# Heads of a packed attention as 64x32 tiles of the matrix array, and two batches in shared sweeps over d_ff

## The chip, the cores and the metric

The kernel runs on one core of one Trainium2 chip. The metric is device time in microseconds (us) of one launch. TensorE (PE) multiplies matrices, and its weight loads are listed apart as PEld; VectorE is DVE, ScalarE is ACT, GpSimd is POOL, and SyncE (SP) issues all DMAs. Each engine works through its own instructions in order, and semaphores hold it back where it needs another engine's result.

## The reference

For each of 8 batches and 8 heads, 32 packed queries `p` attend over 576 keys and values; the result `p'` then serves as key and value for the 576 real queries. The heads are put side by side (8 x 64 = 512 columns) and go through a feed-forward layer with a PReLU.

```python
def sm_attn(qq, kk, vv):                      # head_dim 64, softmax over the last axis
    s = scale * qq @ kk.T
    s = s - max(s); a = exp(s); a = a / (sum(a) + 1e-09)
    return a @ vv
p_packed = sm_attn(p, k, v)                   # 32 x 64 per head
out      = sm_attn(q, p_packed, p_packed)     # 576 x 64 per head
x = out with heads side by side               # 4608 tokens x 512
h = x @ w_in                                  # 512 x 2048, float64 in memory
g = max(h, 0) + alpha * min(h, 0)
return g @ w_out                              # 2048 x 512, float64 in memory
```

## The kernel before

The second attention's weights (576 tokens x 32 packed rows, 8 heads = 256 rows) are called `a`. Since `out @ w_in = a @ (p' w_in)`, the kernel forms `pw = p' w_in` per batch (256 x 2048) and multiplies `a` by it.

**Steps.** A batch's 576 tokens are two halves of 288 columns; `k` = 0 to 15 counts the halves of all batches, `f` = 0 to 15 the blocks of 128 columns of d_ff. A *step* (k, f) is `first` (`ps_h` = `pw` block times `a` half; ACT `neg` = relu(-x), line 401; DVE adds `neg` times (1 - alpha), line 402; ACT copies `gh`, line 407; DVE subtracts `gl`, line 408) and, two steps later, `second`: for each of four output blocks three matmuls into `acc` (lines 420 to 422, `wo` high times `gh`, `wo` low times `gh`, `wo` high times `gl`). This splits a float32 operand into a high and a low float32r part, so that three float32r matmuls stand for one in float32. `first` splits in the same way (lines 395 to 397, six matmuls, after `split_pw` on DVE, lines 371 and 373); for batch 0 (`XF = 1`) it uses two unsplit float32 matmuls (line 383). PE's 256 steps run in the order of the list `order`: first k = 0 and 1 in four sweeps of four f each (sums kept in `part` between sweeps), then k = 2, 3, ... with all 16 f.

**Weights.** `w_out` and `w_in` come as float64 in 32 blocks of 128 x 512 (`wraw`, 512 KB each). `convert` makes float32 of one with two ACT passes and four DVE passes (lines 112 to 126), then splits it with one more pass on each (lines 128, 129). `w_in` is written back, split, as `w_split`, and read again for later batches.

**Attention.** `attention(b, tp)` handles two pairs of heads, as a generator whose stages are called at step numbers given by the list `plan`. Scores (line 188): the stationary matrix holds two heads of a pair on the diagonal of 128 rows x 64 columns with zeros elsewhere (`s1f`, `p2f`); two pairs of heads fill the two halves of the output's 128 partitions. p' (line 258) are matmuls of 128 rows x 64 columns in the same way. `packed_w` (lines 350 to 352) forms `pw` of two batches at once, with 128 x 128 stationary matrices that again hold zeros off the diagonal, split into three float32r matmuls of 512 columns, 16 times; ACT copies the results to `pw`. PSUM is shared out as four banks `acc`, two `ps_h`, and two `ps_m` for everything else.

The scheduler of the framework orders each engine's instructions within what data and buffers allow; the code's order and the step numbers give it the priorities.

Of the kernel before, what the change touches and what calls it, by code (L numbers as in the profile page):

```python
# [16 lines left out]


# [10 lines left out]
def pack_attention_ffn_kernel(  # L29
# [17 lines left out]

# [16 lines left out]
    xin = ctx.enter_context(tc.tile_pool(name="xin", bufs=3))  # L66
    vin = ctx.enter_context(tc.tile_pool(name="vin", bufs=2))
    wk = ctx.enter_context(tc.tile_pool(name="wk", bufs=3))
    sm = ctx.enter_context(tc.tile_pool(name="sm", bufs=4))
    at = ctx.enter_context(tc.tile_pool(name="at", bufs=3))  # L70
    pwp = ctx.enter_context(tc.tile_pool(name="pwp", bufs=8))
    pwj = ctx.enter_context(tc.tile_pool(name="pwj", bufs=2))
    win = ctx.enter_context(tc.tile_pool(name="win", bufs=3))
    gp = ctx.enter_context(tc.tile_pool(name="gp", bufs=2))
# [6 lines left out]
    w_split = dram.tile([NJ, NP, P, 2, 512], F32, name="w_split")  # L81

# [5 lines left out]
    pt = const.tile([P, NP, 2, 2, 64], F32R, name="pt")  # L88
    s1f = const.tile([P, NP, 64], F32, name="s1f")
    p2f = const.tile([P, NP, 64], F32, name="p2f")  # L90
    pt0 = const.tile([P, NP, 2, 2, 64], F32R, name="pt0", tag=f"wo{NF - 1}")
    for t in (s1f, p2f, fv(pt0)):
        nc.gpsimd.memset(t, 0.0)
    wo_t = {}

    XF = 1

    def convert(src, raw, place):

# [3 lines left out]
        mag = xin.tile([P, 512], F32, name="mag", tag="xh")  # L110
        bits = mag.bitcast(U32)
        nc.scalar.activation(out=mag, in_=up, func=AF.Abs)
        low = xin.tile([P, 512], U32, name="low", tag="xl")
# [13 lines left out]
        hi, lo = place()  # L127
        nc.scalar.copy(out=hi, in_=mag)  # L128
        nc.vector.tensor_tensor(out=lo, in0=mag, in1=fv(hi), op=ALU.subtract)  # L129

    def new_raw(f=0):

        if f in left:
            left.remove(f)
            n = f
        elif f == NF - 1:
            n = f
        else:
            n = left.pop(0)
            left.append(n)  # L140
        return const.tile([P, 512], U64, name=f"wraw{n}", tag=f"wo{n}")

    SPARE = 4
    left = list(range(NF - 1 - SPARE, NF - 1))

    def load_w_out(f):
        def place():
            wo_t[f] = const.tile([P, 2, DM], F32R, name=f"wo{f}", tag=f"wo{f}")
            return wo_t[f][:, 0, :], wo_t[f][:, 1, :]

        raw = new_raw(f)
        convert(w_out[f * P : (f + 1) * P, :], raw, place)


    def load_x(src, b, pr):
        if b == 0 and (src is kT or pr == NP - 1):
            n = pr if src is kT else 2 * NP
            raw = const.tile([P, S], F32, name=f"xraw{n}", tag=f"wo{n}")
        else:
            raw = xin.tile([P, S], F32, name="xraw", tag="xraw", bufs=3)  # L160
        nc.sync.dma_start(out=raw, in_=src[b, pr])
        return raw

    def load_v(b, pr):
        if b == 0:
            raw = const.tile([P, KT, P], F32, name=f"vraw{pr}", tag=f"wo{NP + pr}")
        else:
            raw = vin.tile([P, KT, P], F32, name="vraw", tag="vraw")
        nc.gpsimd.memset(raw[: KT * P - S, KT - 1, :], 0.0)
        nc.sync.dma_start(  # L170
            out=raw[:, : KT - 1, :],
            in_=v[b, pr, : (KT - 1) * P].rearrange("(kt kp) d -> kp kt d", kp=P),
        )
        nc.sync.dma_start(out=raw[KT * P - S :, KT - 1, :], in_=v[b, pr, (KT - 1) * P :])
        return raw

    def scores(b, prs, st, xs):

        for hf in range(2):
            sl = slice(hf * HS, hf * HS + HS)  # L180
            if b == 0:
                tag = f"acc{(prs[0] + hf) % 4}"
                ps = ps_a.tile([P, 512], F32, name=tag, tag=tag)
            else:
                ps = ps_m.tile([P, 512], F32, name="ps_m", tag="m")
            for pr, x in zip(prs, xs):
                ro = (pr % 2) * 64
                nc.tensor.matmul(ps[ro : ro + 64, :HS], st[:, pr], x[:, sl], start=True, stop=True)  # L188
            yield hf, sl, ps[:, :HS]

    def new_a(b):
        a_h = at.tile([P, 2, S], F32R, name="a_h", tag="a_h")
        a_l = at.tile([P, 2, S], F32R, name="a_l", tag="a_l", bufs=4)
        result[b] = (a_h, a_l)

    def attention(b, tp):

        ptb, slots = (pt0, (0, 1)) if b == 0 else (pt, (b % 2, b % 2))
        pr0, pr1 = prs = (2 * tp, 2 * tp + 1)
        ts = slice(2 * tp, 2 * tp + 2)
        if tp == 0:
            praw = sm.tile([P, NP, N], F32, name="praw", tag="praw", bufs=1)
            nc.sync.dma_start(out=praw, in_=pT[b])
        k0 = load_x(kT, b, pr0)
        k1 = load_x(kT, b, pr1)
        yield  # L210
        if tp == 0:
            for r in range(2):
                rs, cs = slice(r * 64, r * 64 + 64), slice(r * N, r * N + N)
                nc.scalar.copy(out=s1f[rs, :, cs], in_=praw[rs])
        yield
        s_t = wk.tile([P, S], F32, name="s_t", tag="w")
        for hf, sl, ps in scores(b, prs, s1f, (k0, k1)):
            if hf or b > 0:
                nc.scalar.copy(out=s_t[:, sl], in_=ps)
            else:  # L220
                nc.vector.tensor_copy(out=s_t[:, sl], in_=ps)
        vraw = [load_v(b, pr0)]
# [78 lines left out]
        if b not in result:  # L301
            new_a(b)
# [246 lines left out]
```

## Time and profile before

| | |
|---|---|
| median of 3 runs | 818.55 us (816.24 to 819.24) |
| profiled execution | 816.14 us, its span 814.3 us (1.84 us lie around it) |
| PE clock granted, mean | 0.983 |
| busy: PE, PEld, DVE, ACT, POOL | 775.9, 704.7, 538.5, 412.3, 77.4 us |
| first matmul of line 383, of line 420 | 37.1 us, 49.4 us |
| first matmul of `second` for k = 4 | 290.8 us |
| DMA | 97.95 MB in all; 294 GB/s in the first fortieth of the span |

A row of grouped instructions reads: line, engine, operation, output<-inputs, shape, count, then busy time and mean ns of one. In the shape of a matmul, `128*64` are the rows and columns of the array that it uses, and `128x288` the output. A float32 matmul leaves two records, one for each pass; a float32r matmul and a transpose leave one. The duration of a matmul's record includes its way through the pipeline, so the pace of matmuls is read from start to start. A row of stages (windows) gives the stretch, its length, the busy time and instruction count of each engine, the mean PE clock, the DMA share and GB/s.

### The profile page before, as it was taken

To read this page: it belongs to the slowest core of one execution; us is meant where nothing else is said; L and a number is where in the kernel's file an instruction comes from. 1 tells how busy PE (TensorE), PEld (TensorE's weight loads), DVE (VectorE), ACT (ScalarE), POOL (GpSimd) and SP (SyncE) were. 2 spreads that over 40 slices of the span, in tenths; PEclk is the share of its full clock that TensorE was granted. 3 is DMA by queue.
4 is the path that set the end of the run, shared out by engine and by line. 5 is a ranking of instruction groups with operands and counts; after the bars stand their busy time and mean duration, and the time that the engine had idled before them with its cause. 6 is when DMAs were issued, how large, how long until landed. Compare 5 with 4: busy or idle time off the path is not lost.

```text
span 814.3 us, 14561 instructions
## 1 busy us (share of the span) xinstructions
PE 775.9 (95%) x5456; PEld 704.7 (87%) x5456; DVE 538.5 (66%) x1165; ACT 412.3 (51%) x987; POOL 77.4 (10%) x95
## 2 busy tenths in 40 slices
PE   5599887999999999999999999999999999999997
PEld 3268656888889999899999988889999999999997
DVE  3999998755463468775565568675565566666664
ACT  5688756645547654547335554436435533333332
POOL 1000000025243003012000003010100000000000
PEclk9679999999999999999999999999999999999999
DMA  9887665667446523324303223115303000000000
GB/s 294 289 274 259 217 215 185 200 198 222 143 138 230 192 92 117 91 88 163 126 2 133 81 89 118 59 44 181 108 1 107 2 30 1 30 1 31 1 30 30
DMA packets 55382, 97.95 MB, mean 120 GB/s; under 512 B 5136, under 2 KB 32784, under 8 KB 55312
## 3 DMA queue, kind: packets, MB, share of 16 engines
q1 hardware_dynamic: 55312, 97.02, 36.4%
q8 instruction: 43, 0.70, 0.4%
q14 instruction: 27, 0.22, 0.1%
HBM read 79.18 MB, written 17.83 MB: 119 GB/s over the span
## 4 chain that ended last, share of the span: by engine, by line
PE 84%; DVE 10%; DMA 2%; ACT 2%; issue 1%; SPq 0%; POOL 0%; ACTq 0%; DVEq 0%; POOLq 0%
PE acc L420 16%; PE acc L421 15%; PE acc L422 15%; PE ps_h L395 8%; PE ps_h L397 7%; PE ps_h L396 7%; PE ps_m L188 4%; PE ps_h L383 2%; PE ps_m L258 2%; PE ps_m L352 2%; PE ps_m L351 2%; PE ps_m L350 2%; DVE mag L122 2%; DMA wraw<-in_w_out 2%; DVE mag L126 1%
## 5 line engine op out<-in xcount | busy, mean ns | idle before, releaser
L420 PE MATMUL acc<-gh,wo 128*128 128x288 f32 x1024 | 289.6, 300 | 8.4 <-ACT gh L407 6.6
L421 PE MATMUL acc<-gh,wo 128*128 128x288 f32 x1024 | 285.1, 295 | 0.0
L422 PE MATMUL acc<-gl,wo 128*128 128x288 f32 x1024 | 216.2, 301 | 0.0
L420 PEld LDWEIGHTS acc<-gh,wo 128*128 128x128 f32 x1024 | 192.3, 188 | 22.6 <-ACT gh L407 8.9
L421 PEld LDWEIGHTS acc<-gh,wo 128*128 128x128 f32 x1024 | 192.4, 188 | 2.6 <-issue 0.9
L401 ACT ACTIVATE neg<-ps_h 128x288 f32<-128x288 f32 x256 | 105.1, 412 | 162.6 <-PE ps_h L397 149.7
L408 DVE TENSOR_TENSOR gl<-ps_h,gh 128x288 fp32r<-128x288 f32 x256 | 116.0, 455 | 97.1 <-ACT gh L407 95.5
L402 DVE SCALAR_TENSOR_TENSOR ps_h<-neg,nal,ps_h 128x288 f32<-128x288 f32 x256 | 130.9, 516 | 60.1 <-ACT neg L401 59.5
L407 ACT CAST gh<-ps_h 128x288 fp32r<-128x288 f32 x256 | 102.4, 400 | 133.2 <-DVE ps_h L402 132.0
L422 PEld LDWEIGHTS acc<-gl,wo 128*128 128x128 f32 x1024 | 163.4, 188 | 5.2 <-issue 1.3
L395 PE MATMUL ps_h<-a_h,pwh 128*128 128x288 f32 x448 | 134.3, 300 | 0.0
L397 PE MATMUL ps_h<-a_h,pwl 128*128 128x288 f32 x448 | 132.4, 296 | 0.0
L396 PE MATMUL ps_h<-a_l,pwh 128*128 128x288 f32 x448 | 132.2, 295 | 0.0
L371 DVE CAST pwh<-pw 128x512 fp32r<-128x512 f32 x112 | 51.9, 465 | 65.0 <-PE ps_h L396 64.3
L395 PEld LDWEIGHTS ps_h<-a_h,pwh 128*128 128x128 f32 x448 | 84.0, 188 | 6.2 <-issue 5.0
L397 PEld LDWEIGHTS ps_h<-a_h,pwl 128*128 128x128 f32 x448 | 84.1, 188 | 1.2 <-issue 1.0
L396 PEld LDWEIGHTS ps_h<-a_l,pwh 128*128 128x128 f32 x448 | 84.1, 188 | 0.7 <-issue 0.4
L358 ACT COPY pw<-ps_m 64x512 f32<-64x512 f32 x112 | 65.1, 581 | 23.4 <-PE ps_m L352 16.9
L373 DVE TENSOR_TENSOR pwl<-pw,pwh 128x512 fp32r<-128x512 f32 x96 | 70.2, 732 | 7.9 <-PE ps_h L397 0.3
L383 PE MATMUL ps_h<-a_f,pw 128*128 128x288 f32 x128 | 40.8, 438 | 5.5 <-DVE gl L408 3.4
L352 PE MATMUL ps_m<-w,pt 128*128 128x512 f32 (+1 forms) x80 | 33.7, 424 | 4.4 <-DVE w L129 4.4
L350 PE MATMUL ps_m<-w,pt 128*128 128x512 f32 (+1 forms) x80 | 34.2, 427 | 3.6 <-ACT w L128 3.1
(80 smaller groups left out, 695.2 us busy)
## 6 DMA issues: line engine op xcount, KB each, us to landing
w<-w_split SPq DMA_DIRECT2D x64, 512.0 KB, 4.0
xraw<-in_kT SPq DMA_DIRECT2D x32, 288.0 KB, 3.1
xraw<-in_qT SPq DMA_DIRECT2D x32, 288.0 KB, 3.2
outT<-ot SPq DMA_DIRECT2D x64, 144.0 KB, 1.9
vraw<-in_v SPq DMA_DIRECT2D x32, 256.0 KB, 3.3
wraw<-in_w_out SPq DMA_DIRECT2D x16, 512.0 KB, 4.6
wraw<-in_w_in SPq DMA_DIRECT2D x16, 512.0 KB, 4.8
w_split<-w SPq DMA_DIRECT2D x16, 512.0 KB, 3.7
```

The lines of the kernel that those rows point to most:

```text
L358: nc.scalar.copy(out=pw[b, j][ro : ro + 64, pr // 2, :], in_=ps[i * 64 : i * 64 + 64, :])
L373: eng.tensor_tensor(out=tl, in0=src, in1=fv(th), op=ALU.subtract)
L395: nc.tensor.matmul(ps[:, :HS], th[:, i, fs], a_h[:, i, tok], start=hi, stop=False)
L396: nc.tensor.matmul(ps[:, :HS], th[:, i, fs], a_l[:, i, tok], start=False, stop=False)
L397: nc.tensor.matmul(ps[:, :HS], tl[:, i, fs], a_h[:, i, tok], start=False, stop=lo)
L401: nc.scalar.activation(out=neg, in_=g, func=AF.Relu, scale=-1.0)
L402: nc.vector.scalar_tensor_tensor(out=g, in0=neg, scalar=nal[:, f : f + 1], in1=g, op0=ALU.mult, op1=ALU.add)
L407: nc.scalar.copy(out=gh, in_=g)
L408: nc.vector.tensor_tensor(out=gl, in0=g, in1=fv(gh), op=ALU.subtract)
L420: nc.tensor.matmul(acc[o][:, :HS], wo_t[f][:, 0, os_], gh, start=begin, stop=False)
L421: nc.tensor.matmul(acc[o][:, :HS], wo_t[f][:, 1, os_], gh, start=False, stop=False)
L422: nc.tensor.matmul(acc[o][:, :HS], wo_t[f][:, 0, os_], gl, start=False, stop=end)
```

## The change

- **Heads as tiles.** The stationary matrices hold no zeros any more: each head is a tile of 64 rows (its head_dim) and 32 columns (its packed rows). `heads()` runs through eight of them; row half `r` goes to PSUM bank `r`, and pair `pr` to the 32 partitions `pr`. Scores (now line 193) and `packed_w` (line 306) are eight such matmuls each. p' (line 252) is 128 rows x 32 columns with 64 output columns, four side by side. Batches are handled whole, so `attention(b)` has no `tp`.
- **p' w_in in float32.** `packed_w` makes one float32 matmul of 512 columns per head, one batch at a time, in place of three float32r matmuls; `w_in` is kept unsplit (`w_whole`, 256 KB a block). Zero-filled tiles, splits of p' and of `w_in` and the ACT copies of halves fall away; the softmax's 1/sum is applied in the copy of p' (line 256).
- **Sweeps.** Batches 0 and 1 (k = 0 to 3) now share four sweeps of four f: 64 steps. For both, `first` multiplies unsplit in float32 (`XF = 2`, line 345). Sums stay in `part` for four k; the `at` ring (tag `a`, 7 buffers) holds `part` and `a` alike.
- **Order.** Ahead of the steps, `go` calls stages of attention 0 and 1 (`a`, `b`) and conversions of `w_in` (`i`) in a written order. A string `CONV` gives one conversion or one `packed_w` of batches 0 and 1 to each of the first 35 steps; a later batch's attention takes one stage a step from step 32(b-1)+2 on, and its `packed_w` follows from 32(b-1)+21 on. What is called in a step is placed behind that step's last matmul of `first`, `neg` and line 360 (`issue_after`). `split_pw` is on DVE alone. Pools get more buffers.

```diff
+    def heads():
+        for pr in range(NP):
+            for r in range(2):
+                yield pr, r, slice(r * 64, r * 64 + 64), slice(pr * N, pr * N + N)
-    def scores(b, prs, st, xs):
-        for hf in range(2):
...
-            for pr, x in zip(prs, xs):
-                ro = (pr % 2) * 64
-                nc.tensor.matmul(ps[ro : ro + 64, :HS], st[:, pr], x[:, sl], start=True, stop=True)
+    def scores(b, st, xs, hf):
...
+        for pr, r, rs, cs in heads():
+            nc.tensor.matmul(
+                banks[r][cs, :HS], st[rs, cs], xs[pr][rs, hf * HS : hf * HS + HS],
+                start=True, stop=True,
+            )
...
+            for kt in range(KT):
+                for pr in range(NP):
+                    cs = slice(pr * N, pr * N + N)
+                    nc.tensor.matmul(
+                        ps[cs, rs], aT[:, kt, r, cs], vs[pr][:, kt, rs],
+                        start=(kt == 0), stop=(kt == KT - 1),
+                    )
+            nc.scalar.activation(out=c[:, rs], in_=ps[:, rs], func=AF.Copy, scale=dens[r])
...
+    def packed_w(b, j):
+        banks = [bank() for _ in range(2)]
+        for pr, r, rs, cs in heads():
+            nc.tensor.matmul(
+                banks[r][cs, :], p2[b][rs, cs], wi_t[j, pr][rs, :], start=True, stop=True
+            )
+        pw[b, j] = pwp.tile([P, 2, 512], F32, name="pw", tag="pw")
+        for r in range(2):
+            nc.scalar.copy(out=pw[b, j][:, r, :], in_=banks[r])
...
+    XF = 2
+    go("aiiaabiiaaaaabbb")
...
+    go("bbaabb")
+    packed_w(0, 0)
+    drain(a0)
+    SWEEPS = [(f, f + 4) for f in range(0, NF, 4)]
+    order = [(t, f, s) for s in SWEEPS for t in range(4) for f in range(*s)]
+    order += [(k, f, (0, NF)) for k in range(4, 2 * B) for f in range(NF)]
...
+    CONV = "oooo1iiiioooo01iiiioooo01iiii01oooo"
+    add(converted(CONV), [0 + n // 1 for n in range(len(CONV))])
+    add(a1, [n // 2 for n in range(14)])
+    for b in range(2, B):
+        T = 32 * (b - 1)
+        add(attention(b), range(T + 2, T + 2 + 18))
+        add(packed_w_steps(b), [T + 21 + 2 * n for n in range(NJ + 1)])
```

PE, at one block of p' w_in of later batches. Before, for two batches (`pt` holds p' of both), one of 16 such groups of three:

```order
L421 MATMUL acc_4079<-gh,wo_1076 128x288
L422 MATMUL acc_4079<-gl,wo_1076 128x288
L350 MATMUL ps_m<-w,pt 128x512
L351 MATMUL ps_m<-w,pt 128x512
L352 MATMUL ps_m<-w,pt 128x512
L420 MATMUL acc_4076<-gh,wo_1163 128x288
```

And after, for one batch (`p_3214` is its p'), four such places, each with eight tiles:

```order
L355 MATMUL ps_h<-a_h,pwh 128x288
L306 MATMUL ps_m<-w,p_3214 32x512 x8
L377 MATMUL acc_3536<-gh,wo_1265 128x288
L378 MATMUL acc_3536<-gh,wo_1265 128x288
L379 MATMUL acc_3536<-gl,wo_1265 128x288
```

Eight float32 tiles thus stand where three full float32r matmuls stood, in eight groups for two batches instead of 16, with `first` and `second` on either side.

DVE, in the first sweep, where conversions and steps share it. Before:

```order
L402 SCALAR_TENSOR_TENSOR ps_h<-neg,nal,ps_h 128x288
L126 ISA mag<-mag,low 128x1024
L118 TENSOR_SCALAR mag<-mag 128x512
L115 TENSOR_SCALAR mag<-mag 128x512
L408 TENSOR_TENSOR gl<-ps_h,gh 128x288
L122 SCALAR_TENSOR_TENSOR mag<-wraw_541,mag 128x512
L118 TENSOR_SCALAR mag<-mag 128x512
L129 TENSOR_TENSOR w<-mag,w 128x512
L402 SCALAR_TENSOR_TENSOR ps_h<-neg,nal,ps_h 128x288
```

After:

```order
L360 SCALAR_TENSOR_TENSOR ps_h<-neg,nal,ps_h 128x288
L122 TENSOR_SCALAR mag<-mag 128x512
L119 TENSOR_SCALAR mag<-mag 128x512
L367 TENSOR_TENSOR gl<-ps_h,gh 128x288
L126 SCALAR_TENSOR_TENSOR mag<-wraw_852,mag 128x512
L367 TENSOR_TENSOR gl<-ps_h,gh 128x288
L122 TENSOR_SCALAR mag<-mag 128x512
L130 ISA w<-w,low 128x1024
L126 SCALAR_TENSOR_TENSOR mag<-wraw_892,mag 128x512
L360 SCALAR_TENSOR_TENSOR ps_h<-neg,nal,ps_h 128x288
```

The pattern is alike; only the block of `w_in` has lost its last pass (`w<-mag,w`, line 129).

SP's queue before the first step, after the change (`w_whole<-w` waits for a converted block, and `in_qT` behind it is batch 0's):

```order
L160 DMA xraw<-in_kT 128x576 x4
L112 DMA wraw_202<-in_w_in 128x512
L112 DMA wraw_213<-in_w_in 128x512
L160 DMA xraw_249<-in_qT 128x576
L160 DMA xraw_251<-in_qT 128x576
L146 DMA w_whole<-w 128x512
L160 DMA xraw_253<-in_qT 128x576
L160 DMA xraw<-in_qT 128x576
L146 DMA w_whole<-w 128x512
```

Before, batch 0's four `in_qT` stood ahead of every `wraw`; now batch 1's keys and four blocks of `w_in` stand ahead of them.

More of the change, by code (lines that the diff above doesn't have):

```diff
@@ L87, in pack_attention_ffn_kernel, with drain, bank, new_raw @@
     nal = const.tile([P, NF], F32, name="nal")
[L88 to L98, printed above, removed]
+    wo_t, wi_t, p2, result, pw, pj, gs, part, acc, marks = {}, {}, {}, {}, {}, {}, {}, {}, [], []
+    def drain(gen):
+        for _ in gen:
+            pass
+    def bank(tag=None):
+        if tag is None:
+            return ps_m.tile([P, 512], F32, name="ps_m", tag="m")
+        return ps_a.tile([P, 512], F32, name=tag, tag=tag)
+    SPARE = 4
+    left = list(range(NF - 1 - SPARE, NF - 1))
+    def new_raw(f=None):
+        if f in left:
+            left.remove(f)
+            n = f
+        elif f == NF - 1:
+            n = f
+        else:
+            n = left.pop(0)
+            left.append(n)
+        return const.tile([P, 512], U64, name=f"wraw{n}", tag=f"wo{n}")
+    def to_f32(src, raw, mag):
         nc.sync.dma_start(out=raw, in_=src)
@@ L143, in pack_attention_ffn_kernel @@
[L143 to L162, printed above, removed]
@@ new lines, in first @@
+                nc.tensor.matmul(x, th[:, i, fs], a_l[:, i, tok], start=False, stop=False)
+                mm = nc.tensor.matmul(x, tl[:, i, fs], a_h[:, i, tok], start=False, stop=(i == 1))
+        neg = gp.tile([P, HS], F32, name="neg", tag="neg", bufs=2)
+        marks[:] = [
+            mm,
+            nc.scalar.activation(out=neg, in_=x, func=AF.Relu, scale=-1.0),
+            nc.vector.scalar_tensor_tensor(
+                out=x, in0=neg, scalar=nal[:, f : f + 1], in1=x, op0=ALU.mult, op1=ALU.add
+            ),
+        ]
@@ L409, in first, with second @@
+        gh = gp.tile([P, HS], F32R, name="gh", tag="gh")
+        gl = gp.tile([P, HS], F32R, name="gl", tag="gl")
+        nc.scalar.copy(out=gh, in_=x)
+        nc.vector.tensor_tensor(out=gl, in0=x, in1=fv(gh), op=ALU.subtract)
         gs[k, f] = (gh, gl)
[L411 to L412 removed]
+    def second(k, f, sweep):
+        begin, end = f == sweep[0], f == sweep[1] - 1
         if begin:
[L414 to L416 removed]
+            acc[:] = [bank(f"acc{o}") for o in range(NOC)]
@@ L423, in second @@
+            nc.tensor.matmul(ps, wo_t[f][:, 1, os_], gh, start=False, stop=False)
+            nc.tensor.matmul(ps, wo_t[f][:, 0, os_], gl, start=False, stop=end)
             if not end:
                 continue
-            if k < 2 and f == 3:
-                nc.scalar.copy(out=part[k][:, o], in_=acc[o][:, :HS])
-                continue
-            if f == NF - 1:
+            last = sweep[1] == NF
+            if last:
                 to = op.tile([P, HS], F32, name="ot", tag="ot")
             else:
+                if o == 0 and sweep[0] == 0:
+                    part[k] = at.tile([P, NOC, HS], F32, name="part", tag="a")
@@ L503, in pack_attention_ffn_kernel @@
     AHEAD = 2
     for i in range(len(order) + AHEAD):
-        now = [gen for t, gen, n in plan for _ in range(max(1, -n)) if t <= i and (n < 0 or (i - t) % n == 0)]
-        for gen in now[0::2]:
-            next(gen, None)
         if i < len(order):
-            first(*order[i])
-        for gen in now[1::2]:
-            next(gen, None)
+            first(*order[i][:2])
+        with ExitStack() as behind:
+            for mark in marks:
+                behind.enter_context(tc.issue_after(mark.ins))
+            for gen in turns.get(i, []):
+                next(gen, None)
+            for end, gen in drains:
+                if end == i:
+                    drain(gen)
```

478 lines of the change are left out of this document (194 added, 284 removed).

## The prediction

> **What bounds the kernel now.** The page's head and slices come first: which engine is full, and when.
>
> ```profile
> span 814.3 us, 14561 instructions
> ...
> PE 775.9 (95%) x5456; PEld 704.7 (87%) x5456; DVE 538.5 (66%) x1165; ACT 412.3 (51%) x987; POOL 77.4 (10%) x95
> ...
> PE   5599887999999999999999999999999999999997
> ...
> DVE  3999998755463468775565568675565566666664
> ...
> PEclk9679999999999999999999999999999999999999
> ```
>
> PE is full from the eighth slice on (a slice is 20.4 us). Before that DVE is, in slices 2 to 6. So there are three stages, and the table of stages prices each:
>
> ```profile
> 0.00:20.40 20.40, 11.76 (x72) 7.70 (x73) 6.89 (x20) 10.85 (x25) 3.00 (x15) 1.00 0.90 294
> 20.40:47.00 26.60, 15.06 (x41) 7.09 (x39) 26.41 (x56) 17.98 (x36) 0.00 (x0) 0.60 0.80 271
> 47.00:149.40 102.40, 89.14 (x511) 70.14 (x510) 97.22 (x214) 72.91 (x166) 3.70 (x6) 0.97 0.69 235
> ...
> 290.80:474.60 183.80, 183.47 (x1355) 172.14 (x1354) 118.24 (x256) 90.26 (x225) 16.30 (x18) 1.00 0.31 98
> ...
> 659.60:697.70 38.10, 38.10 (x290) 38.10 (x289) 24.41 (x51) 13.59 (x34) 0.00 (x0) 1.00 0.05 17
> 290.80:814.30 523.50, 518.49 (x3835) 494.57 (x3833) 329.60 (x697) 229.95 (x570) 32.86 (x36) 1.00 0.21 67
> ```
>
> Until 47.0 the queue of loads (294 GB/s) and then DVE (26.41 of 26.60) decide. Then, while weights are converted, DVE is busy 97.22 of 102.40 with 214 instructions: 102.40 / 214 = 478 ns each, stalls included. The same stage by line 402, of which there is one a step:
>
> ```profile
> 0.00:47.02 47.02, 0.00 (x0) 0.77 0.84 281
> 47.02:149.40 102.38, 12.20 (x24) 0.97 0.69 235
> ```
>
> So 24 steps took 102.4 us, 4.27 each. Later PE alone decides: 16 steps with nothing beside them (659.6 to 697.7) take 38.1 us, and k = 4 to 7 take 183.8, so two batches' attention and p' w_in cost PE 183.8 - 4 x 38.1 = 31.4 us. From 290.8 on, 523.5 = 12 x 38.1 + 2 x 31.4 + 3.5 at the end.
>
> **What the tiles cost on PE.** The timeline of PE, at four places, and the first `second` of k = 4 (the last row, 290.80):
>
> ```profile
> 54.12 1.13 PE L383 MATMUL ps_h<-a_f,pw 128*128 128x288 f32 x4
> ...
> 360.63 0.29 PE L421 MATMUL acc<-gh,wo 128*128 128x288 f32 x1
> 360.85 1.19 PE L188 MATMUL ps_m<-xraw,p2f 128*64 128x288 f32 x8
> 361.97 0.40 PE L395 MATMUL ps_h<-a_h,pwh 128*128 128x288 f32 x1
> 362.21 0.30 PE L396 MATMUL ps_h<-a_l,pwh 128*128 128x288 f32 x1
> 362.35 0.29 PE L397 MATMUL ps_h<-a_h,pwl 128*128 128x288 f32 x1
> ...
> 353.27 0.30 PE L422 MATMUL acc<-gl,wo 128*128 128x288 f32 x1
> 353.50 1.31 PE L258 MATMUL ps_m<-vraw,aT 128*64 128x128 f32 x20
> 354.74 0.40 PE L395 MATMUL ps_h<-a_h,pwh 128*128 128x288 f32 x1
> 354.98 0.29 PE L396 MATMUL ps_h<-a_l,pwh 128*128 128x288 f32 x1
> ...
> 222.76 0.71 PE L246 MATMUL ps_m<-ident,s_t 128*128 128x128 f32 x5
> 223.23 0.38 PE L420 MATMUL acc<-gh,wo 128*128 128x288 f32 x1
> ...
> 290.80 0.40 PE L420 MATMUL acc<-gh,wo 128*128 128x288 f32 x1
> ```
>
> A float32r matmul of 288 columns starts every 0.131 us (362.21, 362.35). A full float32 record takes 0.242: four last 1.13, the last itself about 0.40, so (1.13 - 0.40) / 3. Eight `128*64` records last 1.19, which is (1.19 - 0.43) / 3 = 0.25, only three such paces after the first: they run in pairs, two column tiles at once. The same holds for line 258: 20 records in 1.31, ten paces of 0.109, 0.055 a record. And each burst of tiles has a price at its edges: from L421 at 360.63 to L396 at 362.21 is 1.58; two full matmuls and four paces account for 0.26 + 0.97; 0.35 remains. For line 258: 1.71 - 0.26 - 1.09 = 0.36. A burst of transposes fits in 5 x 0.11 without such a price.
>
> **The change, part by part.** *Later batches.* No row shows eight tiles at once. The bounds: nothing beyond pairs, as shown; or all eight at one pace. I take all eight, since the shown pairs lose nothing against one. Then one batch costs: scores, four bursts of two passes, 4 x 0.5 = 2.0; p' w_in, 512 columns at 0.242 x 512/288 = 0.43 a pass, 4 x 0.9 = 3.6; p', 20 passes of half of 0.109, 1.1; 11 transposes 1.2; ten bursts by the order (4 scores, 2 p', 4 p' w_in) x 0.35 = 3.5. (The price at a burst's edge is taken over from another tile shape; the transposes, with none, and twice as much bound it, 21 us down or up over six batches.) Sum 11.4, two batches 22.8 against 31.4. ACT's copies and DVE's work shrink too; both lie beside PE there (DVE 118.24 of 183.8), so I count them at nothing.
>
> *First steps.* Batch 1 in float32 costs PE 0.97 - 6 x 0.131 = 0.18 a step; a step of k < 4 is 12 x 0.131 + 4 x 0.242 = 2.54.
>
> *Start.* The sizes of the loads:
>
> ```profile
> xraw<-in_kT SPq DMA_DIRECT2D x32, 288.0 KB, 3.1
> xraw<-in_qT SPq DMA_DIRECT2D x32, 288.0 KB, 3.2
> ...
> vraw<-in_v SPq DMA_DIRECT2D x32, 256.0 KB, 3.3
> ...
> wraw<-in_w_in SPq DMA_DIRECT2D x16, 512.0 KB, 4.8
> ...
> vraw<-in_v SPq DMA_DIRECT2D x32, 32.0 KB, 3.1
> praw<-in_pT SPq DMA_DIRECT2D x8, 64.0 KB, 3.5
> ```
>
> Batch 0's last queries now have 7.2 MB ahead of them on SP's queue (64 KB of p, 1152 KB of k, two w_in blocks 1024, v 1152, p 64, batch 1's k 1152, two blocks 1024, q 1152, one `w_whole` 256), by 294 GB/s 24.5 us; before they had 3.5 MB. The two `w_whole` writes wait for a converted block, and the last two q loads and batch 1's v and q queue behind them; those blocks are converted in the first 15 DVE instructions, well before 24.5, so no extra. Landing and scores to about 27.7; 25 DVE instructions of batch 0's softmax stand between those scores and the first line 360: 25 x 0.478 = 12.0; `first` and relu at a slow clock some 2.3. First line 360 at 42 (before 47.0). Bounds: 38, if the loads overlap better, and 50.
>
> *Sweeps.* From the first line 360 to the 37th the order holds 238 DVE instructions (28 conversions, 36 steps, 24 sums of `part`, the rest of attention 1), of the same mix as the 214: 238 x 0.478 = 113.8. ACT has 170 instructions there, at the stage's 72.91 / 166 = 0.44 us each 75 us, so it isn't the bound. PE's own need in these 36 steps is 36 x 2.54 + 7 blocks of p' w_in x 1.25 + two score bursts of batch 1 (1.7) = 102, below it. Then the conversions are done and PE decides: 28 x 2.54 + 11.4 for batch 2 = 82.5. `a_l` of batch 2 must wait on the `at` ring for batch 0's `a`, free at step 51; POOL waits there, but its order puts batch 2's other work ahead of it and only batch 3's v memsets behind, and step 64, which needs `a_l`, is 13 steps (33 us) off, so nothing.
>
> *Sum.* 42 + 113.8 + 82.5 + 5 (two steps until `second` of k = 4) = 243, against 290.8. Then 12 x 38.1 + 5 batches x 11.4 + 3.5 = 517.7, against 523.5. Span 761. The profiled execution lies 1.84 above its span, 763, and the median of the runs 2.4 above that: 765.
>
> **The Trainium skill beside it.** The trace shows pairs at full pace. TensorE: Matmul & The Clock Gate, Part 3, has nine tiles at 6.32x and sixteen at 10.6x, about 0.68 of the ideal; by that the 5.6 us of scores and p' w_in of a batch would be 8.2, and the sum 16 us higher, an estimate from the page. No run here shows it. The same part says that a weight load overlaps a running matmul only in another group of rows, which speaks against this change: line 252's four tiles share all rows. By that, 80 loads a batch at 143 ns,
>
> ```profile
> L258 PEld LDWEIGHTS ps_m<-vraw,aT 128*64 128x64 f32 x320 | 18.6, 143 | 4.6 <-issue 2.7 <-ACT aT L249 0.8 <-ACT gh L407 0.2
> ```
>
> would take 11 us for 1.1, and the sum would be 825. The trace does not agree: 20 such loads went by within the 1.31 us of their burst; I give it no chance of its own. The same page (Wait — 56ns, not 53.3ns?) gives a floor of 25 ns from start to start and 62 ns where microcode issues; by the latter p' of a batch would take 5.0 and a burst of scores or of p' w_in 1.0, and the sum would be 801, an estimate from the page. That is the second rival below with another floor, and the 0.68 lies within its partial cases.
>
> **Rivals.** *Slower: tiles of different row halves exclude each other, or no more than two run at once.* Place: scores, p' and p' w_in. A batch's serial work is 4 x 16 x 0.242 + 4 x 16 x 0.43 = 43 us; in pairs 21.5 instead of 5.6, and p' 1.1 more: 17 a batch, six batches in PE-bound stages, 102, and 7 more in the sweeps. Time 874. It decides where fewer than three tiles run at once (43/3 = 14.3, about 9 a batch more, which eats the 54). For it: only pairs are shown, and of column tiles alone. Against: they are shown without loss. 6%.
>
> *Issue bound.* The closest sustained pace in the trace is line 258's, 0.055 a record. p' now has 80 records a batch in 1.1 us, scores 16 in 0.5. If 0.055 is a floor: p' 4.4 (+3.3), scores 0.88 (+0.4 x 4), 4.9 a batch, six batches 29: 794. For it: no row is denser. Against: there the array is full anyway, so the row is no proof of a floor. 17%, partial cases included.
>
> *DVE does not bound the sweeps.* Then PE's 102 replaces 113.8, and a quicker start saves 4 more: 749. Against: 97.22 busy of 102.40 with this mix. 10%.
>
> *The gain is taken back.* Of the 54, 40 rest on 36 steps needing 113.8 and not 36 x 4.27 = 154, the pace of a step before. Relu, line 360, `gh` and `gl` of one step still follow each other across ACT and DVE with conversions between, now with one conversion a step; if each step waits as long as before, the time is 805. Against: DVE's idle time in the stage was 5 of 102 us, so it was the work and not the waits. 4%.
>
> **How the numbers follow.** My own case (752 to 780) has 63%. The range 744 to 798 takes in issue bound and the quicker start; left out are pairs (6%) and stretched sweeps (4%), and some of the tails. A measurement of this kernel tells about 0.5% from no change. Faster: my case, issue bound, no DVE bound, stretched: 0.92 after a little off for what I have not seen; within 0.5% 0.02; slower 0.06.
>
> **What would show it.** Right: line 193's eight tiles (16 records) in about 0.9 us, line 306's in 1.3; first `second` of k = 4 near 243; stages of 16 later steps with a half batch near 44; DVE full until about 155, then PE. Wrong: records of line 193 or 306 whose starts come in pairs 0.24 or 0.43 apart; line 252 above 1 us a burst; PE idle in the sweeps for `gh` or `part`.

## The result: 780.1 us, and the profile after

The changed kernel takes 780.09 us (median of 4 runs, 779.59 to 780.67) against 817.95 for the kernel before in the same series: a ratio of 0.9539 (95% interval 0.9519 to 0.9559). Forecast were 765, with 744 to 798 as range. The sign and the range held; the time is 15 us above the number given and at the upper end of the prediction's own case (752 to 780), so several terms were too small. The page's head and slices, after (a slice is now 19.4 us):

```profile
span 777.8 us, 15920 instructions
...
PE 741.6 (95%) x6232; PEld 651.9 (84%) x6232; DVE 509.9 (66%) x1111; ACT 348.0 (45%) x835; POOL 58.0 (7%) x78
...
PE   5579999999999999999999999999999999999997
...
DVE  3669989884763668555765658556675658556663
```

PE is now full for good from the fourth slice on, not the eighth, and has 34 us less to do. Ahead of the first step DVE no longer decides: in the first row of the table below it is busy 14.80 of 27.20 us, and the loads fill the stretch (DMA share 0.97). The table of stages is cut at the first line 360 (47.60), at the 37th (166.70), at the 65th (251.60), and at the first `second` of k = 4 (254.70):

```profile
20.40:47.60 27.20, 17.49 (x194) 9.11 (x194) 14.80 (x35) 10.52 (x27) 0.73 (x4) 0.62 0.97 334
47.60:166.70 119.10, 110.08 (x720) 86.23 (x705) 110.83 (x238) 77.18 (x170) 5.14 (x4) 0.97 0.49 156
166.70:251.60 84.90, 84.90 (x658) 69.97 (x658) 46.52 (x112) 33.23 (x81) 8.13 (x10) 1.00 0.36 114
254.70:699.40 444.70, 440.94 (x3977) 403.49 (x3976) 283.24 (x612) 191.64 (x475) 42.12 (x46) 1.00 0.28 91
699.40:737.50 38.10, 38.10 (x290) 38.10 (x289) 24.44 (x51) 13.59 (x34) 0.00 (x0) 1.00 0.05 17
254.70:777.80 523.10, 515.06 (x4535) 477.37 (x4533) 328.65 (x704) 217.69 (x540) 42.12 (x46) 1.00 0.25 81
```

| | forecast | measured | difference |
|---|---|---|---|
| first line 360 | 42 | 47.6 | +5.6 |
| 36 steps with conversions | 113.8 | 119.1 | +5.3 |
| 28 steps with batch 2 | 82.5 | 84.9 | +2.4 |
| on to `second` of k = 4 | 5 | 3.1 | -1.9 |
| from there to the end | 517.7 | 523.1 | +5.4 |
| span | 761 | 777.8 | +16.8 |
| median above the span | 4.2 | 2.3 | -1.9 |

The stretch from k = 4 to the end is as long as before (523.10 against 523.50), but the attention of five batches lies in it and not of four. The gain stands ahead of it: `second` of k = 4 begins at 254.70 and not at 290.80.

**The tiles.** PE's timeline around a burst of scores, of p' and of p' w_in (start, us from first start to last end, line, count):

```profile
283.87 0.29 PE L354 MATMUL ps_h<-a_l,pwh 128*128 128x288 f32 x1
284.10 0.72 PE L193 MATMUL ps_m<-xraw,p 64*32 64x288 f32 x16
284.74 0.40 PE L355 MATMUL ps_h<-a_h,pwl 128*128 128x288 f32 x1
284.98 0.55 PE L379 MATMUL acc<-gl,wo 128*128 128x288 f32 x3
...
273.23 0.29 PE L379 MATMUL acc<-gl,wo 128*128 128x288 f32 x1
273.45 0.77 PE L252 MATMUL ps_m<-vraw,aT 128*32 128x64 f32 x40
274.15 0.40 PE L353 MATMUL ps_h<-a_h,pwh 128*128 128x288 f32 x1
274.39 0.29 PE L354 MATMUL ps_h<-a_l,pwh 128*128 128x288 f32 x1
...
330.34 0.29 PE L355 MATMUL ps_h<-a_h,pwl 128*128 128x288 f32 x1
330.56 1.09 PE L306 MATMUL ps_m<-w,p 64*32 64x512 f32 x16
331.58 0.40 PE L377 MATMUL acc<-gh,wo 128*128 128x288 f32 x1
331.81 0.29 PE L378 MATMUL acc<-gh,wo 128*128 128x288 f32 x1
```

Read as in the prediction, from the full matmul ahead of the burst to the second one behind it and less two paces of 0.131: scores 1.11 - 0.26 = 0.85, p' 1.16 - 0.26 = 0.90, p' w_in 1.47 - 0.26 = 1.21. The forecast had 0.85, 0.90 and 1.25. Single records of the burst at 330.56 (start us, ns of one) show why:

```
330.556   613   L306        first of eight, first float32 pass
330.563   613   L306
...
330.603   613   L306        eighth
331.010   589   L306        first of eight, second pass
...
331.056   589   L306        eighth
331.576   401   L377
```

A *pass* is here one of the two records of a float32 matmul. Eight tiles start 7 ns apart and run together; the second pass follows 0.454 us after the first, where the prediction's scaling gave 0.43 for a full record of 512 columns. The Trainium skill, TensorE: Matmul & The Clock Gate, Part 3, models such a pack as one matmul and some 4 ns for each further tile. The trace agrees in kind, with 7 ns.

### The profile page after: what moved, and what is told of

Its sections match the earlier page's. It is cut to its first block, busy times and chain, and to the rows that moved or that the text cites. A ratio compares the mean times of both kernels' runs of the same rounds, so it can differ in the third digit from the quotient of the medians.

```text
span 777.8 us, 15920 instructions
## 1 busy us (share of the span) xinstructions
PE 741.6 (95%) x6232; PEld 651.9 (84%) x6232; DVE 509.9 (66%) x1111; ACT 348.0 (45%) x835; POOL 58.0 (7%) x78
## 4 chain that ended last, share of the span: by engine, by line
PE 82%; DVE 8%; DMA 3%; ACT 3%; issue 2%; SPq 1%; POOL 1%; ACTq 0%; DVEq 0%
PE acc L379 16%; PE acc L377 16%; PE acc L378 15%; PE ps_h L345 7%; PE ps_h L353 7%; PE ps_h L355 6%; PE ps_h L354 6%; PE ps_m L306 5%; PE ps_m L193 2%; DMA vraw<-in_v 2%; PE ps_m L252 1%; DVE ps_h L360 1%; PE ps_m L235 1%; DVE pwl L334 1%; DMA wraw<-in_w_in 1%
## 5 line engine op out<-in xcount | busy, mean ns | idle before, releaser
L377 PE MATMUL acc<-gh,wo 128*128 128x288 f32 x1024 | 295.4, 302 | 7.1 <-ACT gh L366 3.4
L378 PE MATMUL acc<-gh,wo 128*128 128x288 f32 x1024 | 292.3, 296 | 2.6 <-DVE wo L139 2.6
L379 PE MATMUL acc<-gl,wo 128*128 128x288 f32 x1024 | 253.5, 305 | 0.0
L353 PE MATMUL ps_h<-a_h,pwh 128*128 128x288 f32 x384 | 115.1, 300 | 1.9 <-DVE gl L367 1.7
L355 PE MATMUL ps_h<-a_h,pwl 128*128 128x288 f32 x384 | 114.2, 297 | 0.0
L354 PE MATMUL ps_h<-a_l,pwh 128*128 128x288 f32 x384 | 113.2, 295 | 0.0
L345 PE MATMUL ps_h<-a_f,pw 128*128 128x288 f32 x256 | 76.5, 425 | 1.5 <-DVE gl L367 1.2
L355 PEld LDWEIGHTS ps_h<-a_h,pwl 128*128 128x128 f32 x384 | 72.1, 188 | 2.8 <-issue 2.3
L345 PEld LDWEIGHTS ps_h<-a_f,pw 128*128 128x128 f32 x256 | 46.5, 197 | 14.3 <-ACT pw L311 2.1
L306 PE MATMUL ps_m<-w,p 64*32 64x512 f32 x512 | 41.3, 615 | 0.0
L311 ACT COPY pw<-ps_m 128x512 f32<-128x512 f32 x64 | 34.8, 597 | 3.7 <-PE ps_m L306 3.5
```

The lines of the kernel that those rows point to most:

```text
L306: nc.tensor.matmul(banks[r][cs, :], p2[b][rs, cs], wi_t[j, pr][rs, :], start=True, stop=True)
L345: mm = nc.tensor.matmul(x, th[:, i, fs], a_f[:, i, tok], start=(i == 0), stop=(i == 1))
L353: nc.tensor.matmul(x, th[:, i, fs], a_h[:, i, tok], start=(i == 0), stop=False)
L354: nc.tensor.matmul(x, th[:, i, fs], a_l[:, i, tok], start=False, stop=False)
L355: mm = nc.tensor.matmul(x, tl[:, i, fs], a_h[:, i, tok], start=False, stop=(i == 1))
L377: nc.tensor.matmul(ps, wo_t[f][:, 0, os_], gh, start=begin, stop=False)
```

## The experiments

Ratios are to the kernel before (818 to 817 us, run beside them); differences in us are between medians, against the 780.09 of the changed kernel. No run undoes the written order ahead of the steps, `issue_after` or the larger pools alone. Line numbers are those of the changed kernel unless said otherwise.

### Four tiles in place of eight

The second attention's p' is laid out with zeros in the other head's rows, 128 rows x 32 columns, so that only four tiles stand side by side in its scores and in p' w_in.

```diff
-        p2[b] = sm.tile([P, P], F32, name="p2", tag="p2")
-        nc.scalar.copy(out=p2[b], in_=ps[:, :P])
+        p2[b] = sm.tile([P, 2, P], F32, name="p2", tag="p2", bufs=2)
+        for r in range(2):
+            rs, no = slice(r * 64, r * 64 + 64), slice(64 - r * 64, 128 - r * 64)
+            nc.gpsimd.memset(p2[b][no, r, :], 0.0)
+            nc.scalar.copy(out=p2[b][rs, r, :], in_=ps[rs, :P])
...
-                banks[r][cs, :], p2[b][rs, cs], wi_t[j, pr][rs, :], start=True, stop=True
+                banks[r][cs, :], p2[b][:, r, cs], wi_t[j, pr], start=True, stop=True
```

> p' in the second scores and in p' w_in as 128 rows x 32 columns with zeros in the other head's rows: four tiles side by side where eight were. Theory (eight tiles run at the pace of one, PE decides from step 36 on): 4 x 2 x 0.43 + 2 x 2 x 0.242 = 4.4 us more for each of batches 2 to 7, 26, and 7 blocks of p' w_in in the sweeps, up to 7 more: 806 to 813. Rival (row halves don't overlap, or PE has room): under 785.

Measured: 814.06 us (813.83 to 814.75), ratio 0.9967 (0.9954 to 0.9980): 34.0 us slower than the changed kernel, just above the 806 to 813 expected. The group of p' w_in of this kernel (its line 311), and of the changed one:

```profile
L311 PE MATMUL ps_m<-w,p 128*32 128x512 f32 x512 | 68.0, 606 | 0.0
```
```profile
L306 PE MATMUL ps_m<-w,p 64*32 64x512 f32 x512 | 41.3, 615 | 0.0
```

The same 512 records, about as long each (606 and 615 ns), lie in 68.0 instead of 41.3 us: in fours. A burst of p' w_in has four passes, 0.43 apart, instead of two, and takes 2.07 us instead of 1.21; one of the second scores takes 1.33 instead of 0.85. Per batch that is 4 x 2 x 0.43 + 2 x 2 x 0.242 = 4.4, and for eight batches 35. Nearly all of the change's 38 us would be gone with half the tiles.

### Sweeps over one batch, as before

```diff
-    order = [(t, f, s) for s in SWEEPS for t in range(4) for f in range(*s)]
-    order += [(k, f, (0, NF)) for k in range(4, 2 * B) for f in range(NF)]
+    order = [(t, f, s) for s in SWEEPS for t in range(2) for f in range(*s)]
+    order += [(k, f, (0, NF)) for k in range(2, 2 * B) for f in range(NF)]
...
-    add(converted(CONV), [0 + n // 1 for n in range(len(CONV))])
+    add(converted(CONV), [n * 3 // 4 for n in range(len(CONV))])
```

`CONV` becomes `"oooo1" + "iiii01oooo" * 3`, four conversions in three steps.

> The sweeps hold two halves (batch 0) as before the change, 32 steps; batch 1 follows with all 16 f; conversions four in every three steps. Theory (DVE's work sets it, and a sweep of four halves only moves PE's work beside it): 213 DVE instructions to step 26 at 0.50 are 107 us, then 38 steps of PE at 2.54 and batch 2's 11, so 214 instead of 204 us, about 790. Rival (the shared sweeps are where the gain came from): back to 4.27 us a step in the sweeps and near 815.

Measured: 808.42 (805.71 to 812.77), ratio 0.9891 (0.9848 to 0.9934): 28.3 slower, nearer to the rival. Its stages and PE's longest wait up to 185. The stages run from the first line 360 to the 25th, and to the 65th:

```profile
48.80:160.80 112.00, 92.49 (x530) 62.01 (x514) 91.87 (x196) 62.60 (x132) 5.29 (x4) 0.95 0.49 157
160.80:278.00 117.20, 113.28 (x845) 96.99 (x846) 60.14 (x131) 48.52 (x118) 8.16 (x10) 0.97 0.28 92
```
```profile
PE acc L377 <- ACT wo L138: 9.2, 5, 4.8
```

To the 65th step it needs 229.2, the changed kernel 204.0; 25 of the 28 us lie there. PE has too little to do while weights are converted: 24 steps instead of 36 in about the same time. DVE does not fill that time either (91.87 of 112): PE's largest wait is for converted `w_out` (9.2 us, line 377 for line 138). The parts overlap, so 34 and 28 are not to be added; each is what is lost when it alone goes.

### Two small parts undone

`w_in` split again (one ACT and one DVE pass more for each block, nothing else):

```diff
+            hi = cv.tile([P, 512], F32R, name="hi", tag="low")
+            lo = cv.tile([P, 512], F32R, name="lo", tag="mag")
+            nc.scalar.copy(out=hi, in_=w)
+            nc.vector.tensor_tensor(out=lo, in0=w, in1=fv(hi), op=ALU.subtract)
```

> One ACT pass and one DVE pass that split each block of w_in are put back; nothing reads their result. Theory (DVE's work sets the first 36 steps): 12 more DVE instructions there at 0.50, 6 us more, 786. Rival (the removed passes were hidden): no change, 780.

Measured: 784.80 (783.96 to 786.96), ratio 0.9601 (0.9576 to 0.9626), +4.7. In its profile the first line 360 comes at 49.4 instead of 47.6, and the 64 steps take 209.5 instead of 204.0. And batch 1's `first` in split float32r instead of float32 (`XF = 1`, with buffers moved to make room):

> Batch 1's first matmuls split into float32r again (XF = 1, one more buffer in the at ring, two fewer for w_in). Theory (DVE bound): 20 more DVE instructions in the first 36 steps are 10 us, PE saves 0.18 us on 14 later steps, 2.5: about 787. Rival (PE bound in the sweeps): PE saves 0.18 on 32 steps, 5.8: about 774.

Measured: 785.99 (785.74 to 787.15), ratio 0.9614 (0.9593 to 0.9636), +5.9. A step of batch 1 then needs 0.18 us less of PE, and DVE has its `split_pw` to do; PE's waits from 47.6 to 251 grew from 9.0 us in all to 16.8. Both runs agree with the theory that ACT's and DVE's work in the sweeps counts.

### Does DVE's amount of work set the 36 steps?

`CONV` spread over 47 steps, with the steps that have no conversion marked `-`:

```diff
-    CONV = "oooo1iiiioooo01iiiioooo01iiii01oooo"
+    CONV = "oooo1iiii-o01ooo-i-i-ii-oo01o-o-i-i-i-i-oo01o-o"
```

> The conversions of the sweeps are spread over 47 steps instead of 35 (8 a sweep after the first). Theory (DVE's work while converting sets the first 36 steps, 119 us for 238 instructions, 0.50 each, and PE waits): the 64 sweep steps need 52 + 44 + 50 + 46 = 192 us instead of the 204 measured, so about 768 us. Rival (each step is held up by its chain over ACT and DVE, not by the amount of work): no change, 780.

Measured: 779.04 (778.46 to 780.09), ratio 0.9531 (0.9505 to 0.9556), 1.0 below the changed kernel and not told apart from it. The theory fell. Stages of that kernel, first line 360 to the 37th, and to the 65th:

```profile
48.20:158.70 110.50, 103.32 (x686) 84.69 (x671) 97.95 (x211) 66.58 (x151) 5.14 (x4) 0.98 0.42 133
158.70:250.50 91.80, 91.80 (x692) 71.08 (x692) 60.48 (x139) 43.65 (x101) 8.79 (x10) 1.00 0.45 148
```

27 DVE instructions fewer make the 36 steps 8.6 us shorter, as a DVE bound would have it. But PE is busy throughout the next stage, and the work moved there makes it 6.9 longer. Over the 64 steps it is 202.3 against 204.0. In the prediction's words PE's need was 102 in the first stage and 82.5 in the next: by that estimate the 19.5 us between 204.0 and those 184.5 are all that a better order of the 64 steps can win.

Next, PE's order written out: each `first` behind the `second` that the code has ahead of it, for 64 steps.

```diff
+            with ExitStack() as forced:
+                if lastmm and i < 64:
+                    forced.enter_context(tc.issue_after(lastmm[0].ins))
+                first(*order[i][:2])
...
+            with ExitStack() as behind:
+                if i < 64:
+                    behind.enter_context(tc.issue_after(mine.ins))
+                second(*order[i - AHEAD])
```

> In the 64 sweep steps PE's order is held to first of a step, then second of two steps earlier; 63 runs of float32 matmuls there instead of 61. It is the base of the next two. Theory and rival: within 3 us of 780.

Measured: 776.83 (776.55 to 777.29), ratio 0.9508 (0.9494 to 0.9522), 3.3 faster, just beyond the 3 expected. The 65th line 360 stands at 248.1 (first at 48.0): 200.1 for the 64 steps. PE's waits in the sweeps (47.6 to 251), after and then with the order forced (what waits, for what: us in total, times, longest):

```profile
PE acc L377 <- ACT gh L366: 3.4, 4, 1.1
PE acc L378 <- DVE wo L139: 2.6, 2, 1.5
PE acc L377 <- ACT wo L138: 1.4, 1, 1.4
PE ps_h L345 <- DVE gl L367: 1.2, 2, 0.9
```
```profile
PE acc L378 <- DVE wo L139: 3.2, 2, 1.6
PE acc L377 <- ACT wo L138: 3.1, 2, 1.7
PE ps_h L345 <- DVE gl L367: 1.7, 3, 0.9
```

The waits for `gh` are gone, those for converted `w_out` grew from 4.0 to 6.3: 8.2 us in all (with smaller rows) for 9.0. That is 0.8 of the 3.9 us that the 64 steps became shorter. The rest is less busy time of PE with as many instructions; a wait can hide in the busy time (see *A batch* below), and which places became shorter is not settled.

Two more were tried on top of the forced order. In one, the two float32 matmuls of a step stand apart, with six float32r matmuls between, so that the kind changes 125 times instead of 63:

> As the forced order, but the two float32 matmuls of a step stand apart, with half of second between them: 125 runs of float32 matmuls instead of 63. Theory (the matmul behind a float32 one takes 0.217 us more, on PE's path through all sweeps): 62 x 0.217, 13 us above the forced order. Rival (PE has that much room in the sweeps, DVE decides): under 4 us above it.

Measured: 778.27 (777.53 to 778.45), ratio 0.9522 (0.9506 to 0.9538): 1.4 above the forced order, not 13. The theory fell. It came from starts such as these of that kernel (its lines 348 and 383 are 345 and 377):

```profile
119.69 0.65 PE L348 MATMUL ps_h<-a_f,pw 128*128 128x288 f32 x2
119.96 0.51 PE L383 MATMUL acc<-gh,wo 128*128 128x288 f32 x1
120.31 0.30 PE L384 MATMUL acc<-gh,wo 128*128 128x288 f32 x1
```

The float32r record at 119.96 starts early and the next one late (0.35), but from 119.69 to 120.31 are 0.62, and 2 x 0.242 + 0.131 is 0.615. It is the way the records are drawn, and no price of that size. In the other, `first` of two steps stands together, so that the kind changes 34 times (the ring of `gh` and `gl` gets a fourth buffer, the ring of `w` one less):

> As the forced order, but first of two steps stand together: 34 runs of float32 matmuls instead of 63; one more buffer for gh and gl, one fewer for w_in. Theory (0.217 us an edge): 6 us below the forced order, less what PE then waits for gl of both steps while weights are converted. Rival (that wait decides: both ps_h banks come free at once and 3.1 us of second must cover two chains of relu, line 360, gh and gl): at the forced order or above.

Measured: 782.67 (781.77 to 782.99), ratio 0.9577 (0.9563 to 0.9591): 5.8 slower than the forced order. PE's waits there, same stretch:

```profile
PE acc L377 <- ACT wo L138: 5.2, 1, 5.2
PE ps_h L345 <- DVE gl L367: 4.8, 8, 1.4
```

Two `first` in a row need both `ps_h` banks at once, and wait until DVE has read them (4.8 us in eight waits). The other 5.2 us are one wait for converted `w_out`; whether the ring with one buffer less made it so long is not shown.

### The terms that were too small

*Start.* DVE's row before the softmax of batch 0's second attention, its end, and the first line 360; then PE and ACT between the last two (in brackets: idle time before, and what ended it):

```profile
30.17 0.17 DVE L414 TENSOR_SCALAR nal<-al 128x16 f32<-128x16 f32 x1 [5.26 <-DMA al<-in_alpha]
...
39.37 1.43 DVE L291 STREAM_TRANSPOSE a_f<-t 128x576 f32<-128x576 f32 x2
47.61 0.52 DVE L360 SCALAR_TENSOR_TENSOR ps_h<-neg,nal,ps_h 128x288 f32<-128x288 f32 x1 [6.81 <-ACT neg L359]
```
```profile
41.16 2.36 PE L306 MATMUL ps_m<-w,p 64*32 64x512 f32 x16
43.88 3.25 PE L345 MATMUL ps_h<-a_f,pw 128*128 128x288 f32 x6 [0.36 <-ACT pw L311]
...
43.24 1.07 ACT L311 COPY pw<-ps_m 128x512 f32<-128x512 f32 x2 [1.70 <-PE ps_m L306]
```

Two reasons offered themselves. `nal` waits 5.3 us for alpha's load, which is issued behind batch 1's v, and holds up all of DVE's queue. And `packed_w(0, 0)`, on which the first step depends, stands at 41.16, at a granted clock of 0.62 in this stage. First alpha alone, ahead of all loads:

```diff
+    nc.sync.dma_start(out=al, in_=alpha)
+    nc.vector.tensor_scalar(out=nal, in0=al, scalar1=-1.0, scalar2=1.0, op0=ALU.mult, op1=ALU.add)
     go("aiiaabiiaaaaabbb")
-    nc.sync.dma_start(out=al, in_=alpha)
-    nc.vector.tensor_scalar(out=nal, in0=al, scalar1=-1.0, scalar2=1.0, op0=ALU.mult, op1=ALU.add)
```

> Alpha's load and `nal` are issued first of all instead of behind batch 1's v. Theory (the first line 360 is late at 47.6 because DVE's softmax queues behind `nal`, which waits 5.3 us for alpha's load, while the scores were ready at 27.8): softmax starts at about 27.8 instead of 30.2, the first line 360 comes 2.4 us earlier, near 45.2, and the time is near 777.7. Rival (the load queue and PE's slow start decide, or the sweeps swallow it): line 360 stays within 0.5 us of 47.6, the time within 0.8 us of 780.1.

Measured: 779.34 (778.95 to 781.23), ratio 0.9539 (0.9525 to 0.9553): the rival. DVE there:

```profile
30.17 0.75 DVE L218 TENSOR_REDUCE nmx<-s_t 128x1 f32<-128x576 f32 x1 [3.14 <-ACT s_t L212]
```

The wait has changed its name and ends at the same time: late is now `s_t` of batch 1, whose maximum stands ahead of batch 0's softmax in DVE's queue. It is not the same wait in both profiles, though: ACT's copies of `s_t` start at 27.82 in the changed kernel and at 29.73 in this one. The loads move that much between profiles. Line 218 starts at 30.26 to 31.45 in the eight kernels here with the same start and alpha late (mean 30.9), and at 30.17, 29.14 and 29.66 in the three with alpha early (mean 29.7; the latter two are below, and they also place `packed_w(0, 0)` earlier). So the early load gives one microsecond there at most, not 2.4, and in the time alone that is not resolved.

*A batch.* A later batch costs 12.7. Its bursts account for 4 x 0.85 + 2 x 0.90 + 4 x 1.21 and 1.2 for the transposes, 11.2. PE's two kinds of waits between k = 4 and 699.4, at every second change of k, are listed with 0.7 us of idle time a batch:

```profile
PE acc L377 <- ACT ot L392: 1.9, 5, 0.6
PE ps_h L353 <- DVE gl L367: 1.7, 4, 0.5
```

Idle time is less than such a wait costs. The first of them on PE's timeline:

```profile
297.87 0.69 PE L379 MATMUL acc<-gl,wo 128*128 128x288 f32 x4
298.88 0.40 PE L377 MATMUL acc<-gh,wo 128*128 128x288 f32 x1 [0.32 <-ACT ot L392]
299.12 0.30 PE L378 MATMUL acc<-gh,wo 128*128 128x288 f32 x1
```

From 297.87 to 299.12 are 1.25 us, where five starts at the pace of the 16 steps alone (38.1 us for 16 x 18 matmuls, 0.132 each) would take 0.66. So the wait listed as 0.32 costs 0.59: the records of the matmuls ahead of it still count as busy, and the second matmul behind it starts 0.24 after the first. The second kind, at 303.04, is listed as 0.46 and costs 0.73. Read so, the ten waits cost 6.4 us, 1.3 a batch, and 11.2 + 1.3 is nearly all of the 12.7. The changes of k in between (the first at 343.6) have no such wait.

At the changes with a wait, ACT and DVE drain `acc` of a finished k and do the softmax of a batch at the same time. So attention of batches 3 to 7 was moved five steps earlier:

```diff
-        add(attention(b), range(T + 2, T + 2 + 18))
+        S0 = T + 2 if b == 2 else T - 3
+        add(attention(b), range(S0, S0 + 18))
```

> Attention of batches 3 to 7 starts five steps earlier, so that its softmax is over before the step at which k changes. Theory (a batch costs 12.7 instead of 11.4 because ACT and DVE do its softmax just where `ot` is drained and the first `gh`, `gl` of the next k are made, and PE waits 0.3 to 0.4 us twice there): five batches give back 1.3 each, time near 773.6, later 32-step stages near 87.6 instead of 88.9. Rival (the stall at the change of k is the drain's own, or moves to where the attention now stands): 779 to 780.5, stages unchanged.

Measured: 783.34 (783.19 to 783.58), ratio 0.9584 (0.9571 to 0.9597), 3.3 slower. Its stage from k = 4 to the end of batch 7's attention, and PE's one wait there:

```profile
260.00:703.20 443.20, 441.42 (x3938) 402.58 (x3936) 295.72 (x602) 188.06 (x464) 40.45 (x46) 1.00 0.27 88
```
```profile
PE acc L377 <- ACT gh L366: 1.3, 5, 0.3
```

PE's idle time (length less busy) fell from 3.8 to 1.8 us and the stage from 444.7 to 443.2, 0.3 a batch and not 1.3. Even that is no gain: two bursts of batch 3's scores, 1.7 us, now lie ahead of k = 4, and that stretch (first line 360 to 260.0) became 211.2 instead of 207.1. Nor did the waits shrink. In the changed kernel 20 starts of a float32r matmul come over 0.16 us after the float32r matmul ahead (bursts left out), here 53, and they cost 7.7 us instead of 6.4. Most of these show no idle time at all:

```profile
291.15 0.29 PE L378 MATMUL acc<-gh,wo 128*128 128x288 f32 x1
291.38 0.40 PE L353 MATMUL ps_h<-a_h,pwh 128*128 128x288 f32 x1
291.62 0.30 PE L354 MATMUL ps_h<-a_l,pwh 128*128 128x288 f32 x1
```

From 291.15 to 291.62 are 0.47 for two paces, 0.26. So the 1.3 of the theory is what the waits cost, but an earlier start does not remove them: as the rival had it, they moved to where the attention now stands. The time is above both forecasts: the first line 360 came 1.2 later, the stretch to k = 4 is 4.1 longer, the rest 1.5 shorter.

*Together.* The forced order, alpha early, the shift, and `packed_w(0, 0)` right behind `go("aiiaabiiaaaaabbb")`:

> Together: forced order of `first` before `second` in the first 64 steps, alpha early, packed_w(0, 0) placed ahead of the second half of batch 1's attention, later attention five steps earlier. Theory (each removes a wait of its own at its own place): -3.3 for the order as run alone, -2.4 for alpha, -2.5 for PE's and ACT's 2.7 us of packed_w(0, 0) that now lie in the path before the first line 360, -6.6 for the shift: near 765.5. Rival (they share one slack: what the sweeps gain at the start is given back before step 64, as the run with spread conversions did): 772 to 777.

Measured: 774.83 (773.77 to 775.72), ratio 0.9479 (0.9466 to 0.9492): within the rival's bounds. The first line 360 of this kernel:

```profile
44.36 0.52 DVE L360 SCALAR_TENSOR_TENSOR ps_h<-neg,nal,ps_h 128x288 f32<-128x288 f32 x1 [3.85 <-ACT neg L359]
```

The wait ahead of it is 3.85 in place of 6.81: 3.0 us were `packed_w(0, 0)` in the path. With the forced order, alpha early or the shift alone it stayed at 6.8. With the spread `CONV` as well:

> As the one before, and the conversions spread over 47 steps. Theory (with the order forced, PE's need and not DVE sets the first 64 steps, and spreading alone was worth 1): within 2 us of the run before, 764 to 766. Rival (spreading removes the remaining stalls of `first` in the first 36 steps that the forced order makes PE wait for): 4 or more below the run before.

Measured: 773.43 (773.07 to 773.87), ratio 0.9462 (0.9450 to 0.9475), 1.4 below the run before: within the 2 us that the theory allowed, though far from its 764 to 766. This is the fastest version that was run, 6.7 us or 0.9% below the changed kernel. The same without the shift, which cost 3.3 alone, was not run.

## Why the prediction was right, and where its terms were too small

- **Later batches: the mechanism right, the price 1.3 short.** "All eight at one pace" holds: passes 0.454 apart, eight starts within 47 ns. The edge price of 0.35, taken from another tile shape, holds for all three kinds (0.85 - 2 x 0.242 = 0.37; 0.90 - 10 x 0.056 = 0.34; 1.21 - 2 x 0.43 = 0.35). The Trainium skill, TensorEngine Tiling (Array Packing), Key Properties, says that a change of the tiling mode drains the engine; it gives no time. The trace shows 0.35 for both edges of a burst; that this is such a drain is not shown. The bursts came to 11.2 a batch, but a batch to (444.7 - 10 x 38.1) / 5 = 12.7 against 11.4. The step that failed was counting ACT's and DVE's work beside PE at nothing: PE's waits for them at the change of k, read from start to start, are 1.3 a batch. Some 0.2 stays open.
- **Start: 5.6 short.** The last scores (line 193 on PE, from 27.36 on) ended at 28.3 (forecast 27.7). DVE went on only at 30.2, since `nal` and batch 1's maxima stand ahead of the softmax (+2.5 in all, at most some 1 of it alpha's); it took 10.6 instead of 12.0 (-1.4); and "`first` and relu at a slow clock some 2.3" measured 6.8 (+4.5). That step left out `packed_w(0, 0)` and its copies, 3.0 of it by the row of the combined run; 1.5 stays open.
- **36 steps: 5.3 short.** 238 instructions were indeed there, at 0.50 and not 0.478: busy 110.83 / 238 = 0.466 (before 97.22 / 214 = 0.454) is 2.7 of it, idle 8.3 where the old share gives 5.8 is 2.5. As an account of that stage the DVE bound held. As the account of the time it did not: the spread run made the stage 8.6 shorter and the time at most some 1 us. What counts is the 64 steps together, and there PE's need of 184.5 plus waits for `gh` and converted weights. So pricing these 36 steps by DVE alone came near in number, but it is not what sets the time.
- **28 steps with batch 2: 2.4 short.** 28 x 2.54 leaves 13.8 of the 84.9 for batch 2 instead of 11.4. No run takes this apart.
- **Rivals.** Tiles in pairs (874) are excluded by the starts and by the run with four tiles, which shows the size of what could have gone. The floor of 0.055 a record (794), and with it the larger one (801 in the prediction, 802 to 803 by its own terms), is excluded: p' has four tiles in 56 ns, 14 ns a record, and eight records of line 306 start in 47 ns. The gain taken back (805): 36 steps at 119.1 and not 154. DVE not the bound (749): its time is excluded, since the start was later and not quicker, and PE was not full in the 36 steps (110.08 of 119.10); its doubt was right, since less DVE work in that stage left the time where it was.
- **The signs named.** Bursts near 0.9 and 1.3, and 16 later steps with half a batch near 44 (88.9 / 2 = 44.5): seen. `second` of k = 4 near 243, DVE full until 155: 254.7, and 8 or 9 tenths to the end of the ninth slice, 175. Of the signs of being wrong one was there in small: PE waited 3.4 us for `gh` in the sweeps.
- **Luck.** The upper end of the range, 798, was drawn for an issue bound (794), which did not come. That the time lies within it is partly luck: the room was taken up by other errors, four terms too small, two of them because work had been left out or counted at nothing.

## What to carry to other kernels

Small float32 matmuls that use a part of the array are worth laying out as tiles side by side as long as their bursts are few: here a burst costs its passes and 0.35 us, with eight tiles of 64 x 32 as with four of 128 x 32. Price a speed-up of a stage by the stages up to the next point at which one engine is full, not by itself; work that is moved out of the crowded stage is paid in the full one. A wait that the profile names may be the last of several: count its removal only down to what is late next in the same queue. And read PE's waits from start to start: listed idle time showed 0.7 us a batch where the waits cost 1.3.

## What the runs showed of the hardware

- Four tiles of 128 x 32 or eight of 64 x 32, both with 512 columns, run a pass in 0.43 to 0.454 us: rows split in two halves take no longer than rows whole. That no row before could tell.
- One after another the 16 records of a p' w_in burst would take 16 x 0.43 = 6.9 us and those of scores 3.9; in tiles of eight they take 1.21 and 0.85, edges and all: 5.7 and 4.6 times less. The 0.68 of the ideal that the prediction took from the Trainium skill, TensorE: Matmul & The Clock Gate, Part 3, would be 5.4 times, an estimate from the page. With the edges counted in, the trace is near it for p' w_in and below it for scores; inside a burst, where eight tiles run a pass in 0.454 us, nothing of that kind is lost. Whether the page's figures hold the edges it does not say; if they do, the 16 us that the prediction worked out from them beside the edge price count the edges twice.
- 62 more changes between float32 and float32r cost 1.4 us, at most some 0.02 each, though records at such a change look as if they cost 0.2.
